# Feed-forward products of 512 tokens with their sums in two PSUM banks, and the chunk outputs of the attention part in the banks of the first product

## The chip, the cores and the metric

The program runs on one core of one Trainium2 chip. A core has TensorE (PE in the profile; its weight loads are listed apart as PEld), VectorE (DVE), ScalarE (ACT), GpSimd (POOL) and SyncE (SP, which issues all DMAs here). The metric is the time of one execution on the device, in microseconds.

## What is computed

A chunked state-space attention over 4 sequences of 768 tokens, with 8 heads of 32 channels, and then a feed-forward layer over the 3072 tokens (256 channels, 2048 hidden), all in float32:

```python
for c in range(nc):
    L = np.exp(cum[:, :, :, None] - cum[:, :, None, :]) * causal
    M = np.einsum('bhin,bhjn->bhij', Cc, Bc) * L
    y[:, :, sl] = einsum(M, xc) + einsum(Cc, state) * exp(cum)
    state = decay_full * state + sum(Bx)
x = y.transpose(0, 2, 1, 3).reshape(B * S, H * D)
h = x @ w_in
g = h - np.tanh(h)
return g @ w_out
```

## The kernel before

**Attention.** The tokens are cut into 28 chunks of up to 112 tokens (7 to a sequence, `CPB`). For each chunk, `chunk_a` makes decays and scores in PSUM (`att`, four banks, lines 452 and 458), ACT takes the exponential (`lt`, L462), DVE multiplies (L466) and POOL masks (L469). `chunk_y` makes the outputs `y` (L494) and the state for the next chunk (L502) in a PSUM bank of its own. ACT copies the state into the next chunk's `x` (L507, four small copies) and y into `xh` (L514), rounded to the type that PE multiplies in one pass; DVE keeps the rest, y - xh, in `xl` (L519).

**Feed-forward.** `TT` = 256 tokens make a window, `t` = 0 to 11. The 2048 hidden channels are eight units `u` of 256, each with its part of w_in and w_out, loaded as 64-bit words and converted by `conv` (five DVE and two ACT operations a unit) into a rounded weight `wh` and a rest `wl` (L321, the last of them). One step is one window with one unit. `mm1` makes `ph`, two blocks of 128 hidden channels by 256 tokens in one bank, as xh·wh + xh·wl + xl·wh over two halves of the 256 channels: 12 matmuls (L545). `act` does tanh (ACT, L559), subtracts (DVE, L563), rounds g to `gh` (ACT, L567) and keeps the rest `gl` (DVE, L574). `mm2` adds gh·wh + gh·wl + gl·wh into `o`, both halves of the output channels in one bank: 12 matmuls again (L595). There are two banks for `ph` (`NPH`), one for `o`, one for `y`, four for `att`: all eight.

**Sweeps.** Windows 0 to 3 go over the units two at a time (`SWEEPS`), because the units come one after another: at the end of a sweep `keep` adds `o` to a partial sum in SBUF (L609; a copy, L616, in the first sweep). Windows 4 to 11 take all eight units in a row. `store` empties the finished `o` (L627 with the partial sum; L629 on ACT and L631 on DVE, one half each, without) and sends it out (L634). That makes 96 steps.

**Order.** Nothing is issued as written. `Order` collects every operation with its engine, a cost and what it reads and writes; `slot` hands out buffers in turn, and an operation waits for those that read the buffer before. `plan` lists the operations by priorities that a seeded search varies, and `issue` emits them in the order of the planned starts, so each engine runs a fixed sequence. "hard" dependencies are waits with a latency, "soft" ones only an order.

Of the kernel before, what the change touches and what calls it, by code (L numbers as in the profile page):

```python
# [10 lines left out]
F32 = mybir.dt.float32  # L11
# [9 lines left out]
P = 128  # L21
# [9 lines left out]
TT = 256  # L31
NT = T // TT
# [12 lines left out]
SWEEPS = 0, 2, 4, 6, 8  # L45


class Order:
# [24 lines left out]
    def __call__(self, eng, cost, fn, r=(), w=(), dma=0, after=()):  # L73
# [134 lines left out]
def tile_ssm_moe(ctx: ExitStack, tc: tile.TileContext, a, x, bn, bc, wts, out):  # L208
# [16 lines left out]

    chunks, ends = {}, 0
    for t in range(NT):
        b, j = divmod(t, S // TT)
        end = b * CPB + -(-(j + 1) * TT // Q)
        chunks[t], ends = list(range(ends, end)), end  # L230
# [4 lines left out]
    SPAN = slice(len(chunks[0]), len(chunks[0]) + 7), slice(len(chunks[0]) + 7, NCK)  # L235
# [49 lines left out]
    wl = cp.tile([P, NCONV, 2, 2, 256], F32R, name="wl")  # L285

# [85 lines left out]
    def first_tile():  # L372
# [39 lines left out]
        for ck in range(len(chunks[0])):  # L412
# [65 lines left out]
    def chunk_y(ck):  # L478
# [4 lines left out]
        n_y = slot("y", 1)  # L483
# [6 lines left out]
        def fn():  # L490
            y = k["y"] = ps_y.tile([P, 2 * H * D], F32, tag="y", name=f"y{ck}")
# [17 lines left out]

        def fn_h():  # L510
            if c == 0:
                seq[b]["xh"] = p3.tile([P, 2, S], F32R, tag="xh", name=f"xh{b}", bufs=2)
            k["yv"] = k["y"][:, 0 : 2 * Q].rearrange("p (g q) -> p g q", g=2)[:, :, 0:q]
            nc.scalar.copy(seq[b]["xh"][:, :, c * Q : c * Q + q], k["yv"])  # L514

        def fn_l():
            if c == 0:
                seq[b]["xl"] = p3.tile([P, 2, S], F32R, tag="xl", name=f"xl{b}", bufs=2)
            nc.vector.tensor_tensor(out=seq[b]["xl"][:, :, c * Q : c * Q + q], in0=k["yv"],  # L519
                                    in1=seq[b]["xh"][:, :, c * Q : c * Q + q].bitcast(F32), op=ALU.subtract)  # L520
# [9 lines left out]
    def mm1(t, u):  # L530
        b, j = divmod(t, S // TT)
        d, ts = seq[b], slice(j * TT, (j + 1) * TT)
        cs = [c for c in range(CPB) if c * Q < ts.stop and (c + 1) * Q > ts.start]
        n_h, n_g = slot("ph", NPH), slot("g", 3)
        gs[t, u, 0] = [n_h, n_g]

        def fn():
            ph = ps_h.tile([P, 2, TT], F32, tag="ph", name=f"ph{t}_{u}")
            gs[t, u] = [ph]
            for j in range(2):  # L540

                for p in range(2):
                    for k in range(2):
                        for w_ in (wh, wl)[: 2 - p]:
                            nc.tensor.matmul(out=ph[:, j, :], lhsT=w_[:, u, 0, k, j * P : (j + 1) * P],  # L545
# [334 lines left out]
```

## Time and profile before

| | us |
|---|---|
| median of three runs | 345.87 |
| lowest and highest run | 345.47, 346.5 |
| span of the profiled execution | 344.3 |
| median less that span | 1.57 |
| busy: ACT | 192.9 |
| busy: POOL | 57.2 |
| mean granted TensorE clock | 0.970 |

The profile is one execution; its own time is not listed apart from its span, so the span is set against the median of the runs. A line of a group names its source line, engine and operation, output and inputs, the shape (partitions x elements) and the count, then busy us and mean ns of one, then the idle time before it and what ended it. Matmuls are pipelined: one lasts about 280 ns from start to end, and the next starts long before, so the pace is the distance of two starts, or a block's time divided by its count. The chain of waits is followed back from the last instruction.

### The profile page before, as it was taken

The numbers are of one execution on the slowest core, as the hardware profiler recorded it, in microseconds if no ns is written. First come the engines' busy times: TensorE is split into PE (matmuls) and PEld (weight loads), VectorE is DVE, ScalarE is ACT, GpSimd is POOL, SyncE is SP. The second block draws the span as 40 slices with busy tenths as digits, with TensorE's granted clock in tenths as the row PEclk, the third lists the DMA queues.
The fourth block names the chain that finished last, engine by engine and source line by source line (L and its number), as shares of the span: only waits on it lengthen the run. The fifth ranks groups of instructions, "written<-read, shape, count | busy, mean of one in ns | idle before, by whom it ended". The sixth has DMA issues, their size and how long they took to land.

```text
span 344.3 us, 8873 instructions
## 1 busy us (share of the span) xinstructions
PE 330.2 (96%) x3756; PEld 317.9 (92%) x3756; DVE 227.5 (66%) x339; ACT 192.9 (56%) x403; POOL 57.2 (17%) x69
## 2 busy tenths in 40 slices
PE   7939979999999999999999999999999999999995
PEld 6839879999999999999999999999999999999995
DVE  5996898999998875645654655555655555654552
ACT  7855977786554543534655646444554555554441
POOL 1544453340000110101211110210401110110000
PEclk9875989999999999999999999999999999999999
DMA  7929658614000011001211200200200100000100
GB/s 164 301 63 317 179 131 201 213 52 132 3 0 3 10 51 61 32 3 45 61 45 30 63 2 9 82 2 23 71 2 1 32 2 2 32 0 2 32 0 31
DMA packets 12471, 21.39 MB, mean 62 GB/s; under 512 B 2848, under 2 KB 7648, under 8 KB 12432
## 3 DMA queue, kind: packets, MB, share of 16 engines
q1 hardware_dynamic: 12432, 20.84, 21.4%
q8 instruction: 29, 0.48, 0.6%
q14 instruction: 10, 0.08, 0.1%
HBM read 17.51 MB, written 3.32 MB: 60 GB/s over the span
## 4 chain that ended last, share of the span: by engine, by line
PE 87%; DVE 3%; SPq 3%; DMA 3%; ACT 1%; issue 1%; POOL 0%; POOLq 0%; DVEq 0%; ACTq 0%
PE o L595 40%; PE ph L545 38%; PE y L494 3%; PE att L458 2%; DMA braw<-bn_d 2%; PE cp L381 1%; DMA bc<-bc_d 1%; PE att L452 1%; SPq L770 1%; SPq L278 1%; SPq L247 1%; PE y L502 1%; PE att L392 1%; DVE wm L310 0%; SPq L772 0%
## 5 line engine op out<-in xcount | busy, mean ns | idle before, releaser
L559 ACT ACTIVATE g<-ph 128x512 f32<-128x512 f32 x96 | 57.4, 598 | 91.5 <-PE ph L545 89.3
L563 DVE TENSOR_TENSOR g<-ph,g 128x512 f32<-128x512 f32 x96 | 65.9, 690 | 62.9 <-ACT g L559 62.9
L545 PE MATMUL ph<-xh,wh 128*128 128x256 f32 x384 | 101.3, 286 | 0.0
L545 PE MATMUL ph<-xh,wl 128*128 128x256 f32 x384 | 100.0, 283 | 0.0
L574 DVE TENSOR_TENSOR gl<-g,gh 128x512 fp32r<-128x512 f32 x96 | 67.0, 700 | 26.9 <-ACT gh L567 25.7
L545 PE MATMUL ph<-xl,wh 128*128 128x256 f32 x384 | 77.1, 282 | 0.0
L567 ACT CAST gh<-g 128x512 fp32r<-128x512 f32 x96 | 59.1, 619 | 28.7 <-DVE g L563 27.2
L545 PEld LDWEIGHTS ph<-xh,wh 128*128 128x128 f32 x384 | 73.8, 192 | 1.1 <-issue 0.4
L545 PEld LDWEIGHTS ph<-xh,wl 128*128 128x128 f32 x384 | 73.8, 192 | 0.0
L469 POOL TENSOR_SCALAR_AFFINE_SELECT lt<-lt 128x896 f32<-128x896 f32 (+1 forms) x25 | 34.0, 1359 | 203.9 <-DVE lt L466 203.9
L595 PE MATMUL o<-gh,wh 128*128 128x256 f32 x384 | 63.5, 287 | 0.0
L595 PE MATMUL o<-gl,wh 128*128 128x256 f32 x384 | 60.2, 278 | 0.0
L595 PE MATMUL o<-gh,wl 128*128 128x256 f32 x384 | 60.2, 278 | 0.0
L545 PEld LDWEIGHTS ph<-xl,wh 128*128 128x128 f32 x384 | 59.8, 192 | 0.0
L595 PEld LDWEIGHTS o<-gh,wh 128*128 128x128 f32 x384 | 51.2, 188 | 2.8
L595 PEld LDWEIGHTS o<-gl,wh 128*128 128x128 f32 x384 | 51.5, 188 | 0.0
L595 PEld LDWEIGHTS o<-gh,wl 128*128 128x128 f32 x384 | 51.5, 188 | 0.0
L466 DVE TENSOR_TENSOR lt<-att,lt 128x896 f32<-128x896 f32 (+1 forms) x25 | 26.7, 1067 | 6.8 <-ACT lt L462 6.8
L462 ACT ACTIVATE lt<-att 128x896 f32<-128x896 f32 (+1 forms) x25 | 22.6, 902 | 6.1 <-PE att L458 4.4
L507 ACT COPY x<-y 16x64 f32<-16x64 f32 x96 | 19.4, 202 | 8.6 <-DVE xl L519 7.1
L494 PE MATMUL y<-lt,x 128*32 128x112 f32 (+1 forms) x448 | 17.3, 274 | 5.4 <-POOL bc L352 3.3
L494 PEld LDWEIGHTS y<-lt,x 128*32 128x32 f32 x448 | 10.2, 113 | 9.2 <-POOL bc L352 3.4
(70 smaller groups left out, 232.8 us busy)
## 6 DMA issues: line engine op xcount, KB each, us to landing
raw<-w_d SPq DMA_DIRECT2D x16, 512.0 KB
x<-x_d SPq DMA_DIRECT2D x14, 256.0 KB
bc<-bc_d SPq DMA_DIRECT2D x56, 60.0 KB
out_d<-ob SPq DMA_DIRECT2D x24, 128.0 KB
braw<-bn_d SPq DMA_DIRECT2D x14, 112.0 KB
cum<-parts SPq DMA_DIRECT2D x1, 168.0 KB
rt_c<-cum SPq DMA_DIRECT2D x4, 27.0 KB
lt_c<-cum SPq DMA_DIRECT2D x4, 27.0 KB
```

The lines of the kernel that those rows point to most:

```text
L458: nc.tensor.matmul(out=at_[:, i, 2 + w, :], lhsT=bb[r, w], rhs=cc[r, w, 0:q], start=True, stop=True)
L462: nc.scalar.activation(k["l"][:, :, 0:q].rearrange("p (i w) q -> p i w q", i=4), k["a"][:, :, 0:2, :], AF.Exp)
L466: nc.vector.tensor_tensor(out=lt, in0=k["a"][:, :, 2:4, :], in1=lt, op=ALU.mult)
L469: nc.gpsimd.affine_select(out=k["l"][:, :, 0:q], in_=k["l"][:, :, 0:q], pattern=[[0, H], [1, q]], compare_op=ALU.is_ge, fill=0.0, base=N, ...
L494: nc.tensor.matmul(out=y[D * h : D * h + D, hg * Q : hg * Q + q], lhsT=d["x"][:, cg, P * hg + D * h : P * hg + D * h + D], rhs=k["l"][:, 4 ...
L507: nc.scalar.copy(grp[(ck + 1) // CPG]["x"][0:N, (ck + 1) % CPG, 2 * D * i : 2 * D * i + 2 * D], k["y"][D * i : D * i + N, H * D : H * D + ...
L545: nc.tensor.matmul(out=ph[:, j, :], lhsT=w_[:, u, 0, k, j * P : (j + 1) * P], rhs=d[("xh", "xl")[p]][:, k, ts], start=p == 0 and k == 0 an ...
L559: nc.scalar.activation(g, gs[t, u][0], AF.Tanh)
L563: nc.vector.tensor_tensor(out=g, in0=ph, in1=g, op=ALU.subtract)
L567: nc.scalar.copy(gh, gs[t, u][1])
L574: on.tensor_tensor(out=gl, in0=g, in1=gh.bitcast(F32), op=ALU.subtract)
L595: nc.tensor.matmul(out=po[t, seg][:, e, :], lhsT=w_[:, u, 1, j, e * P : (e + 1) * P], rhs=g[:, j, :], start=u == seg[0] and k == 0 and j = ...
```

## The change

Only the first sweep keeps windows of 256 tokens (`NARROW` = 1): 4 windows by 2 units, 8 steps. Everything else uses six windows of `TW` = 512 tokens. A wide step is one window with one block of 128 hidden channels, `f` = 0 to 15, so `ph` is still one bank: 128x512 instead of two blocks of 128x256. `mm1` and `mm2` of a wide step are 6 matmuls each. The sums of a wide window need two banks, one for each half of the output: the bank of `o` and the bank that `y` had, now also called `oe`. Chunks 10 to 27, which are not needed by the first 1024 tokens, therefore put `y` into one of the two banks of `ph`. A wide window crosses a sequence's end, so `xh` and `xl` become one tile each, with room for two sequences. Partial sums and outputs follow: two reads of 512 columns, on DVE for partial sums, on ACT and DVE without, and outputs of 256 KB instead of 128. In `Order`, a DMA that writes what another DMA wrote is now also ordered (soft) behind that DMA's issue.

```diff
-NT = T // TT
+TW = 512
+NARROW = 1
...
                 if dma and self.ops[j][0] == "DMA":
                     chain.add(j)
+                    soft.add(j - 1)
...
+    narrow = [(t * TT, TT) for t in range(NSW)]
+    wide = [(t * TW, TW) for t in range(T // TW)]
...
+    early = range(next(iter(chunks[wide[NSW * TT // TW]])))
...
+    xh = cp.tile([P, 2, 2 * S], F32R, name="xh")
+    xl = cp.tile([P, 2, 2 * S], F32R, name="xl")
...
-        n_y = slot("y", 1)
+        n_y = slot("y", 1) if ck in early else slot("ph", NPH)
...
-            y = k["y"] = ps_y.tile([P, 2 * H * D], F32, tag="y", name=f"y{ck}")
+            pool, tag = (ps_y, "y") if ck in early else (ps_h, "ph")
+            y = k["y"] = pool.tile([P, 2 * H * D], F32, tag=tag, name=f"y{ck}")
...
-    def mm1(t, u):
+    def mm1(w, f):
...
+        u, ts = f // 2, slice(at % (2 * S), at % (2 * S) + n)
+        blocks = range(f % 2, f % 2 + TW // n)
...
-            ph = ps_h.tile([P, 2, TT], F32, tag="ph", name=f"ph{t}_{u}")
-            for j in range(2):
+            ph = ps_h.tile([P, TW // n, n], F32, tag="ph", name=f"ph{at}_{f}")
+            for j in blocks:
...
-        op("PE", 1.41, fn, r=[*[d["n_xh"][c] for c in cs], *[d["n_xl"][c] for c in cs], f"wh{u}.0", f"wl{u}.0"], w=[n_h])
+        op("PE", 1.41 if n == TT else 1.32, fn,
...
-            n_po[t, seg] = slot("po", 1)
+            n_po[w, seg] = [slot("po", 1)] if n == TT else [slot("po", 1), slot("y", 1)]
...
+                    po[w, seg] = (ps_o.tile([P, TW], F32, tag="po", name=f"o{at}_{f}"),
+                                  ps_y.tile([P, TW], F32, tag="y", name=f"oe{at}_{f}"))
...
+        if n == TW:
+            for e in range(2):
+                op("DVE", 0.69, lambda e=e: nc.vector.tensor_tensor(out=partial(w)[:, e], in0=po[w, seg][e], in1=partial(w)[:, e], op=ALU.add),
...
+            for e in range(2):
+                op("DVE" if summed or e else "ACT", 0.69 if summed else 0.6, lambda e=e: fn_c(e),
...
-            op("SP", 0.42, lambda i=i: fn_d(i), r=[name[i]], dma=KB)
+            op("SP", 0.42, lambda e=e: fn_d(e), r=[name[e]], dma=KB * n // TT)
...
-    segs = [(t, tuple(range(i, j))) for i, j in zip(SWEEPS, SWEEPS[1:]) for t in range(NSW)]
-    segs += [(t, tuple(range(NCONV))) for t in range(NSW, NT)]
+    for s, (i, j) in enumerate(zip(SWEEPS, SWEEPS[1:])):
+        for w in narrow if s < NARROW else wide[: NSW * TT // TW]:
+            segs.append((w, tuple(range(2 * i, 2 * j, TW // w[1]))))
+    segs += [(w, tuple(range(NF))) for w in wide[NSW * TT // TW :]]
```

In these names a number behind ph, o, g, gh and gl is the window and the unit before (ph5_7 is window 5, unit 7), and the first token and the block f of the change (ph1024_7 is tokens 1024 to 1535, block 7); y16, lt16 and att17 are chunks; the last number only counts tiles. On PE, around the y of chunk 16, in the kernel before:

```order
L545 MATMUL ph5_7_2616<-xl1_797,wh_83 128x256 x2
L494 MATMUL y16_2633<-lt16_2579,x8_1208 32x112 x8
L502 MATMUL y16_2633<-x8_1208,bw8_1210 16x32 x8
L595 MATMUL o5_0_2414<-gh5_5_2582,wh_83 128x256 x4
L595 MATMUL o5_0_2414<-gh5_5_2582,wl_84 128x256 x4
L595 MATMUL o5_0_2414<-gl5_5_2598,wh_83 128x256 x4
L452 LDWEIGHTS lt_c_104
L452 MATMUL att17_2672<-rt_c_105,lt_c_104 128x224
```

There y16 has its own bank and stands between the end of a product and an o block of 12 matmuls. In the change, the same place on PE, from the last two matmuls of a product on:

```order
L553 MATMUL ph1024_7_1985<-xl_86,wh_83 128x512 x2
L502 MATMUL y16_1994<-lt16_1671,x8_1276 32x112 x8
L510 MATMUL y16_1994<-x8_1276,bw8_1278 16x32 x8
L611 MATMUL o1024_0_1876<-gh1024_5_1972,wh_83 128x512
L611 MATMUL oe1024_0_1877<-gh1024_5_1972,wh_83 128x512
L611 MATMUL o1024_0_1876<-gh1024_5_1972,wl_84 128x512
L611 MATMUL oe1024_0_1877<-gh1024_5_1972,wl_84 128x512
L611 MATMUL o1024_0_1876<-gl1024_5_1980,wh_83 128x512
L611 MATMUL oe1024_0_1877<-gl1024_5_1980,wh_83 128x512
L553 MATMUL ph1024_8_2028<-xh_85,wh_83 128x512
```

The o block is now six matmuls that alternate between the banks o and oe, and the product that follows it, ph1024_8, takes the ph bank of ph1024_7, since y16 holds the other one. The end of that product and what comes next on PE:

```order
L553 MATMUL ph1024_8_2028<-xl_86,wh_83 128x512 x2
L611 MATMUL o1024_0_1876<-gh1024_6_1992,wh_83 128x512
L611 MATMUL oe1024_0_1877<-gh1024_6_1992,wh_83 128x512
L611 MATMUL o1024_0_1876<-gh1024_6_1992,wl_84 128x512
L611 MATMUL oe1024_0_1877<-gh1024_6_1992,wl_84 128x512
L611 MATMUL o1024_0_1876<-gl1024_6_2011,wh_83 128x512
L611 MATMUL oe1024_0_1877<-gl1024_6_2011,wh_83 128x512
L553 MATMUL ph1024_9_2048<-xh_85,wh_83 128x512
```

So the bank of y16 is asked for again by ph1024_9, behind an o block, a product and another o block.

On DVE, around the last weight split (wl of unit 7, which reads wv7) in the kernel before:

```order
L609 TENSOR_TENSOR pt2_1029<-o2_4_1642,pt2_1029 128x512
L574 TENSOR_TENSOR gl3_5_1690<-g3_5_1655,gh3_5_1673 128x512
L321 TENSOR_TENSOR wl_84<-wv7_1395,wh_83 128x1024
L563 TENSOR_TENSOR g0_6_1705<-ph0_6_1675,g0_6_1705 128x512
L519 TENSOR_TENSOR xl1_797<-y11_1173,xh1_771 128x2x112
L466 TENSOR_TENSOR lt12_1170<-att12_1095,lt12_1170 128x896
L609 TENSOR_TENSOR pt3_1190<-o3_4_1692,pt3_1190 128x512
```

Here the xl of chunk 11 (it reads y11) and the lt of chunk 12 stand behind that split. In the change, on DVE, from the split of unit 6 on:

```order
L328 TENSOR_TENSOR wl_84<-wv6_1152,wh_83 128x1024
L573 TENSOR_TENSOR g512_8_1440<-ph512_8_1420,g512_8_1440 128x512
L309 TENSOR_SCALAR wm7_1452<-raw7_1182 128x1024
L473 TENSOR_TENSOR lt14_1394<-att14_1373,lt14_1394 128x896
L583 TENSOR_TENSOR gl0_10_1485<-g0_10_1386,gh0_10_1417 128x512
```

The lt of chunk 14 has come ahead of the last split, and those of chunks 12 and 13 stand earlier still. A little later on DVE the split of unit 7 itself:

```order
L525 TENSOR_TENSOR xl_86<-y12_1454,xh_85 128x2x112
L314 TENSOR_SCALAR wv7_1296<-wv7_1296 128x1024
L583 TENSOR_TENSOR gl512_9_1539<-g512_9_1504,gh512_9_1529 128x512
L632 TENSOR_TENSOR pt0_607<-o0_8_1432,pt0_607 128x512
L632 TENSOR_TENSOR pt0_607<-oe0_8_1433,pt0_607 128x512
L317 SCALAR_TENSOR_TENSOR wm7_1452<-wv7_1296,wm7_1452 128x1024
L321 SCALAR_TENSOR_TENSOR wv7_1296<-wv7_1296,wm7_1452 128x1024
L573 TENSOR_TENSOR g512_10_1549<-ph512_10_1532,g512_10_1549 128x512
L573 TENSOR_TENSOR g512_11_1562<-ph512_11_1542,g512_11_1562 128x512
L328 TENSOR_TENSOR wl_84<-wv7_1296,wh_83 128x1024
```

The xl of chunk 12 is ahead of it too, and each partial sum (pt) is now two operations, one for o and one for oe. The products of blocks 8 to 11, the third sweep, stand ahead of the split in both kernels.

More of the change, by code (lines that the diff above doesn't have):

```diff
@@ L224, in tile_ssm_moe @@
     raws, gs, po, n_po, obs, misc = {}, {}, {}, {}, {}, {}
+    narrow = [(t * TT, TT) for t in range(NSW)]
+    wide = [(t * TW, TW) for t in range(T // TW)]
     chunks, ends = {}, 0
[L227 to L230, printed above, removed]
+    for w in narrow + wide[NSW * TT // TW :]:
+        b, j = divmod(sum(w) - 1, S)
+        end = b * CPB + j // Q + 1
+        chunks[w], ends = list(range(ends, end)), end
     wv, wm, pts, n_pt = {}, {}, {}, {}
@@ L410, in fn_s @@
                                     fill=0.0, base=N, channel_multiplier=-1)
-        for ck in range(len(chunks[0])):
+        for ck in range(len(chunks[narrow[0]])):
             k = chs[ck]
@@ L567, in fn_h @@
[L567 to L568 removed]
+            gh = p3.tile(shape, F32R, tag="gh", name=f"gh{w[0]}_{f}")
+            nc.scalar.copy(gh, gs[w, f][1])
+            gs[w, f].append(gh)
         def fn_l():
[L571 to L575 removed]
+            _, g, gh = gs[w, f]
@@ L592, in fn @@
             for k, (w_, g) in enumerate(((wh, gh), (wl, gh), (wh, gl))):
-                for j in range(2):
+                for j in blocks:
                     for e in range(2):
-                        nc.tensor.matmul(out=po[t, seg][:, e, :], lhsT=w_[:, u, 1, j, e * P : (e + 1) * P],
-                                         rhs=g[:, j, :], start=u == seg[0] and k == 0 and j == 0 and e == 0,
-                                         stop=u == seg[-1] and k == 2 and j == 1, skip_group_check=True)
@@ L599, in mm2 @@
-        op("PE", 1.41, fn, r=[n_h, n_l, f"wh{u}.1", f"wl{u}.1"], w=[n_po[t, seg]])
-        if u == seg[-1]:
+                        nc.tensor.matmul(out=po[w, seg][e], lhsT=w_[:, u, 1, j, e * P : (e + 1) * P],
+                                         rhs=g[:, j - f % 2, :],
+                                         start=f == seg[0] and k == 0 and j == blocks[0] and (n == TW or e == 0),
+                                         stop=f == seg[-1] and k == 2 and j == blocks[-1], skip_group_check=True)
@@ L608, in keep @@
         if seg[0]:
-            op("DVE", 0.69, lambda: nc.vector.tensor_tensor(out=pts[t], in0=po[t, seg], in1=pts[t], op=ALU.add),
-               r=[n_po[t, seg]], w=[n_pt[t]])
+            op("DVE", 0.69, lambda: nc.vector.tensor_tensor(out=partial(w), in0=po[w, seg][2], in1=partial(w), op=ALU.add),
+               r=n_po[w, seg], w=[n_pt[i, e, half] for e in range(2)])
             return
-        n_pt[t] = slot("pt", NSW)
+        if half == 0:
+            names = op.pieces(slot("pt", NSW * TT // TW), 4)
+            n_pt.update({(i, e, x): names[2 * e + x] for e in range(2) for x in range(2)})
@@ L614, in fn @@
         def fn():
[L615 to L642 removed]
+            if half == 0:
+                pts[i] = p1.tile([P, 2, TW], F32, tag="pt", name=f"pt{i}", bufs=NSW * TT // TW)
@@ L824, in tile_ssm_moe @@
         if g < len(steps):
-            t, u, _ = steps[g]
-            mm1(t, u)
-            act(t, u, "DVE")
+            w, f, _ = steps[g]
+            mm1(w, f)
+            act(w, f)
             for fn, args in todo.get(g, ()):
```

151 lines of the change are left out of this document (83 added, 68 removed).

## The prediction

> **What bounds the kernel now.** I read the busy shares first, then the chain that ended last, then the span in stretches, then the instructions themselves where the bound sits.
>
> ```profile
> span 344.3 us, 8873 instructions
> PE 330.2 (96%) x3756; PEld 317.9 (92%) x3756; DVE 227.5 (66%) x339; ACT 192.9 (56%) x403; POOL 57.2 (17%) x69
> PE 87%; DVE 3%; SPq 3%; DMA 3%; ACT 1%; issue 1%; POOL 0%; POOLq 0%; DVEq 0%; ACTq 0%
> PE o L595 40%; PE ph L545 38%; PE y L494 3%; PE att L458 2%; DMA braw<-bn_d 2%; PE cp L381 1%; DMA bc<-bc_d 1%; PE att L452 1%; SPq L770 1%; SPq L278 1%; SPq L247 1%; PE y L502 1%; PE att L392 1%; DVE wm L310 0%; SPq L772 0%
> ```
>
> TensorE holds 87% of the chain, and the two feed-forward lines (L545 makes ph, L595 adds up o) hold 78% of it. The other engines and the DMA queues appear in the chain only near its start. The stretches show where that changes; each row gives busy us of PE, PEld (weight loads), DVE, ACT and POOL, then the granted clock.
>
> ```profile
> 20.00:30.00 10.00, 6.49 (x85) 5.75 (x85) 8.06 (x10) 4.79 (x13) 4.71 (x4) 0.54 0.54 166
> 50.00:60.00 10.00, 10.00 (x160) 9.42 (x159) 7.96 (x12) 6.66 (x17) 4.26 (x5) 0.93 0.74 177
> 60.00:75.00 15.00, 15.00 (x206) 14.16 (x205) 14.64 (x19) 11.62 (x26) 6.00 (x7) 1.00 0.43 134
> 75.00:118.00 43.00, 43.00 (x382) 43.00 (x381) 40.02 (x56) 24.32 (x42) 2.17 (x2) 1.00 0.11 35
> 118.00:200.00 82.00, 82.00 (x911) 79.64 (x914) 47.38 (x71) 41.36 (x87) 9.42 (x11) 1.00 0.14 42
> 200.00:340.70 140.70, 140.70 (x1556) 136.47 (x1548) 76.06 (x113) 70.76 (x145) 14.86 (x14) 1.00 0.06 18
> ```
>
> From 50 us to the last matmul PE has no idle time, and from 60 us its clock is full. Two kinds of stretch follow. From 60 to 118 us DVE is nearly as full as PE: 14.64 + 40.02 = 54.66 of 58 us, because it still converts weights. After 118 us DVE is at 54 to 58%, and PE alone decides. So what a PE instruction costs there is worth its full price.
>
> A busy PE says nothing of its pace; the chain's blocks do. One block is one product (mm1 or mm2) of one step, 12 matmuls of 256 columns.
>
> ```profile
> 78.89 1.36 PE o L595 x12
> ...
> 291.15 0.21 PE att L452 x4
> 291.35 0.45 PE att L458 x16
> 291.80 1.61 PE o L595 x12
> 293.41 1.41 PE ph L545 x12
> ...
> 297.65 0.52 PE y L494 x16
> 298.17 0.12 PE y L502 x16
> ```
>
> There are two paces: 1.36 / 12 = 113.3 ns and 1.41 / 12 = 117.5 ns per matmul. The chain's pieces from 75 us on hold 58 blocks of the first kind and 83 of the second, and 29 that follow attention work and pay about 0.2 us more (1.61 at 291.80). Mean of the first two kinds: (58 x 1.36 + 83 x 1.41) / 141 = 1.39 us, **116 ns per matmul, 232 ns per two**.
>
> **The change, part by part.** *Width.* Of the 96 steps, the 8 of the first sweep stay at 256 tokens; 88 become wide. Each had 24 matmuls of 256 columns and now has 12 of 512: 88 x 12 = 1056 pairs become one matmul each, with one weight load instead of two. The trace has no matmul of 512 columns. The lower bound of its time comes from a place where the clock was half.
>
> ```profile
> 49.00:51.20 2.20, 2.20 (x12) 2.20 (x12) 2.02 (x2) 1.22 (x5) 1.25 (x1) 0.50 0.14 38
> ...
> 48.99 0.42 PE L545 MATMUL ph<-xh,wl 128*128 128x256 f32 x1
> 49.21 0.41 PE L545 MATMUL ph<-xh,wh 128*128 128x256 f32 x1
> 49.42 0.41 PE L545 MATMUL ph<-xh,wl 128*128 128x256 f32 x1
> 49.63 0.63 PE L545 MATMUL ph<-xl,wh 128*128 128x256 f32 x2
> ```
>
> At clock 0.50 the same matmuls start (49.63 - 48.99) / 3 = 213 ns apart. If that is the stream of 256 columns alone, it takes 107 ns at the full clock, and the 113 to 118 measured there hold 6 to 11 ns of something else. What that is decides the price, and another row points at the weight load:
>
> ```profile
> 5.15 1.04 PE L381 MATMUL cp<-upto,la 128*128 128x112 f32 x8
> ```
>
> Here, at clock 1.00, eight matmuls of only 112 columns with the same 128x128 weights take 1.04 us; less the length of one (0.33 us, the group's mean), seven starts lie about 0.10 to 0.11 us apart. They are less than half as wide, and no faster. So I take it that near 110 ns the weight load sets the pace, that at 256 columns load and stream nearly tie, and that at 512 the stream stands alone. **Bounds for one wide matmul: 213 ns (stream alone) and 232 ns (as two now, no gain).** The half-clock rows are the nearest: they too stream for twice as long beside one load of the same weights. I take 216, 3 ns above them, since a full-clock pace never came down to its stream. Saving: 1056 x (232 - 216) = **-16.9 us**; by the bounds -20 and 0.
>
> The Trainium skill ("TensorE: Matmul & The Clock Gate", Back-to-back issue gap) gives a warm, isolated matmul N/2.4 + 2.5 ns, an estimate of 216 at 512 columns, by which the sum above would be the same. But the same rule gives 109 at 256: by it alone a pair costs 218 and the change saves 2.5 ns a pair, 2.6 us in all. This trace's 113 to 118 do not agree with that 109.
>
> *DVE in the sweeps.* Tanh, subtractions and casts stay as many and as long, 128x512 each:
>
> ```profile
> L563 DVE TENSOR_TENSOR g<-ph,g 128x512 f32<-128x512 f32 x96 | 65.9, 690 | 62.9 <-ACT g L559 62.9
> L574 DVE TENSOR_TENSOR gl<-g,gh 128x512 fp32r<-128x512 f32 x96 | 67.0, 700 | 26.9 <-ACT gh L567 25.7
> L466 DVE TENSOR_TENSOR lt<-att,lt 128x896 f32<-128x896 f32 x21 | 22.9, 1088 | 6.4 <-ACT lt L462 6.4
> L519 DVE TENSOR_TENSOR xl<-y,xh 128x224 fp32r<-128x224 f32 x24 | 9.3, 389 | 5.0 <-ACT x L507 3.8 <-ACT xh L514 1.1
> ```
>
> So DVE cannot follow where it is full. Between 60 us and the last weight split (unit 7) lie the sweeps over units 2 to 5, 16 steps: PE would gain 16 x 12 x 16 ns = 3.1 us. But the new order also puts the lt products of chunks 12 to 14 and the xl of chunks 11 and 12 ahead of that split on DVE (the order rows of the change show the last of them), which stood behind it: about 3 x 1.09 + 2 x 0.39 = 4.0 us, against the 58 - 54.7 = 3.3 us that DVE idles there. At best the split comes 0.7 us later than now, with about 2.0 us of PE's attention work done early (att of chunks 13 and 14 at 0.21 + 0.45, y of chunk 12 at 0.52 + 0.12, by the chain's rows above). So of the 3.1 us only 1.3 is realised, **+1.8**; if DVE keeps its idle time, +5.1. I take the first, since the planner has more to fill it with: **+2**.
>
> *y in the product banks.* 18 of the 28 chunks (10 to 27) put y into one of the two ph banks, and hold it until the last reader:
>
> ```profile
> 297.58 0.59 PE L494 MATMUL y<-lt,x 128*32 128x112 f32 x16
> 297.74 0.60 ACT L559 ACTIVATE g<-ph 128x512 f32<-128x512 f32 x1 [0.58 <-PE ph L545]
> 297.99 0.30 PE L502 MATMUL y<-x,bw 128*16 128x32 f32 x16
> 298.21 0.72 PE L595 MATMUL o<-gh,wh 128*128 128x256 f32 x4
> 298.37 0.69 DVE L563 TENSOR_TENSOR g<-ph,g 128x512 f32<-128x512 f32 x1 [0.48 <-ACT g L559]
> 298.61 0.41 ACT L507 COPY x<-y 16x64 f32<-16x64 f32 x2
> 299.05 0.39 DVE L519 TENSOR_TENSOR xl<-y,xh 128x224 fp32r<-128x224 f32 x1
> 299.48 0.20 ACT L507 COPY x<-y 16x64 f32<-16x64 f32 x1 [0.46 <-DVE xl L519]
> ```
>
> PE leaves y at about 298.29 and its last copy ends at 299.68, 1.4 us later. In the new order y is followed by an o block, a ph block into the other bank, and another o block before its own bank is wanted: about 3.9 us, enough. Tighter is the ph block right after: it wants the bank of the product ahead of y, which is read until tanh and subtraction are done, 299.06 against that product's end near 297.6: 1.5 us, where y and one o block give 0.64 + 1.30 = 1.94. Slack 0.4 us, unless another ACT or DVE instruction (lt, 0.9 to 1.1 us) stands ahead. Bounds: 0, and 18 x 0.7 = 12; behind a waiting matmul stands all of PE. I take the lower end's side, because this slack is positive: **+1.5** for this and for the sums below.
>
> *Two banks for the sum.* Fewer sums are emptied (14 instead of 24), each by two reads of 512 columns (0.69 us on DVE) instead of one of both halves. Most of the changeovers have two product blocks between the last and the next o block, 2.6 us of cover; where one stands there (1.3 us), the second bank is ready up to 0.3 us late. This is inside the 1.5.
>
> *The end.* The order still ends with four o blocks without a product.
>
> ```profile
> 335.11 5.67 PE o L595 x48
> 340.80 0.38 ACT ob L629
> 341.20 0.42 DVE ob L631
> ...
> GB/s 0 0 0 33 0 0 0 0 0 0 0 0 0 0 0 0 0 0 0 0 0 0 0 0 0 0 0 0 0 0 0 0 0 0 260 264 16 0 0 0
> ```
>
> Now ACT and DVE copy half each of one bank, one behind the other, 0.82 us; then two copies of twice the size from two banks can run together, 0.69. The last 256 KB moved at about 260 GB/s in slices of 0.5 us; 512 KB take 1.0 us more. **+1**.
>
> *Start.* The new soft rule on DMA writers reorders SP's queue and with it the first 50 us. PE idles 3.5 of 10 us between 20 and 30 us there, so it can go either way; I take 0, with 3 us to both sides.
>
> **Sum.** 344.3 - 16.9 + 2 + 1.5 + 1 = 331.9 us of span. The median of the runs, 345.87, is 1.6 above the profiled span; so **333.5 us**.
>
> **Rivals.** *A fixed price per matmul.* If the 6 to 7 ns over the stream at the faster pace belong to every matmul, a wide one takes 220, the saving falls by 1056 x 4 = 4.2 us: **337.7**. For it: the 113.3 recurs over long stretches. Against: the half-clock rows have no such part.
>
> *The price is in the columns.* If a wide matmul costs what two narrow ones do, 232, the 4.5 us of costs remain: **350.4**, slower. Point of decision: above 228 ns per wide matmul (4.5 / 1056 = 4 ns saved). The 112-column row speaks against it, as does the change of pace between 113 and 118 at equal columns. By the Trainium skill's fixed 2.5 ns (same page and section) this rival would save 2.6 us and end at 347.8.
>
> *The product banks become the bound.* If ACT serves y late, so that each of the 18 y costs PE the 1.4 us to its last reader, that is 25 us: 332.0 + 25 = **357**, slower. It decides from 13.9 / 18 = 0.8 us per y, twice the slack. For it: with y in a ph bank one bank is left for products. Against: ACT and DVE are half idle there (41.36 and 47.38 of 82 us).
>
> *DVE keeps its idle time in the sweeps, or the start is unlucky*: +3, **336.8**.
>
> **Chances.** Forecast 0.53; fixed price 0.24; DVE or start 0.12; columns 0.06; banks 0.05. The first three are faster, 0.89, and I leave 0.03 for the banks or columns ending within 0.3% of 345.87 (1.0 us, about what a measurement of this kernel can tell from no change), so 0.08 slower. Range: the forecast with 213 ns and a lucky start goes to 329; the fixed price with 3 us of bad start to 341. That leaves out columns, banks and a little of each tail.
>
> **What would show it.** The chain's blocks: six wide matmuls in 1.30 us (216), 1.32 (220) or 1.39 (no gain), with rows of 128x512 on L553 and L611. PE idle between 75 us and the end, with DVE ahead of it before unit 7's split, or with the readers of y behind ph. The time from the last o block to the end, 3.5 us now, at 4.5. I am wrong if blocks take over 1.37, if the granted clock falls under 1.00 after 60 us, or if PE idles over 5 us there.

## The result, and the profile after

| | before | after |
|---|---|---|
| median, us (17 runs each) | 344.55 | 346.68 |
| lowest and highest run, us | 343.66, 346.67 | 345.37, 348.91 |
| span of the profiled execution, us | 344.3 | 345.0 |

The ratio of the times is 1.0063, with a 95% interval of 1.0039 to 1.0087: the change makes the kernel slower by about 2 us, 0.6%. The forecast was 333.5 us with a range of 329 to 341, so it was wrong, in sign and size. The page of the kernel after, its first rows and its chain by engine and line:

```profile
span 345.0 us, 6725 instructions
PE 326.9 (95%) x2700; PEld 264.6 (77%) x2700; DVE 229.4 (66%) x335; ACT 194.6 (56%) x399; POOL 55.4 (16%) x69
PE 86%; DVE 5%; DMA 4%; ACT 2%; issue 1%; SPq 1%; ACTq 0%
PE ph L553 39%; PE o L611 21%; PE oe L611 18%; PE y L502 4%; PE att L465 3%; DMA x<-x_d 2%; DMA raw<-w_d 2%; PE att L459 1%; DVE lt L473 1%; DVE g L573 1%; ACT x L515 1%; DVE wl L328 1%; PE y L510 1%; DVE rt_c L437 1%; DVE wm L317 1%
```

PE has 1056 instructions less (2700 for 3756) and 53 us less of weight loads, but it is busy for 326.9 us instead of 330.2, and the two feed-forward lines still hold 78% of the chain. The weight loads that went had lain beside the matmuls. The stretches of the kernel after (length, then busy us and instructions of PE, PEld, DVE, ACT, POOL, then the granted clock):

```profile
20.00:60.00 40.00, 33.48 (x533) 30.34 (x533) 37.65 (x46) 28.03 (x61) 19.62 (x19) 0.83 0.67 185
60.00:75.00 15.00, 13.80 (x151) 12.39 (x152) 14.91 (x20) 11.63 (x25) 4.58 (x4) 1.00 0.45 137
75.00:118.00 43.00, 43.00 (x293) 33.63 (x292) 38.44 (x53) 26.01 (x47) 5.05 (x6) 1.00 0.16 46
118.00:200.00 82.00, 82.00 (x623) 64.72 (x622) 48.67 (x73) 42.09 (x89) 10.20 (x12) 1.00 0.11 35
200.00:341.00 141.00, 140.74 (x922) 111.36 (x920) 74.76 (x111) 69.28 (x134) 9.48 (x10) 1.00 0.05 16
```

From 75 us on PE idles for 141.00 - 140.74 = 0.26 us in all, at full clock, as before. So nothing new holds PE up there; what PE does there takes as long as it did. Blocks of one wide product in the chain, six matmuls each:

```profile
310.28 1.39 PE ph L553 x6
313.06 1.39 PE ph L553 x6
315.83 1.39 PE ph L553 x6
318.60 1.39 PE ph L553 x6
```

1.39 / 6 = 232 ns for one wide matmul; the mean distance of two starts, over 978 of them after 75 us (those across or right behind small matmuls are left out), is 230.8 ns. Two narrow ones cost 231.9 in the trace of before by the same count (115.97 over 2013). So a wide one saves 1.1 ns, not 16, and 1056 of them save **1.2 us**.

Two smaller places changed. Between 60 and 75 us PE now idles 1.20 us, where it was full. The rows around the second sweep's first product show it, in the timelines of after and of before:

```profile
65.07 0.68 DVE L573 TENSOR_TENSOR g<-ph,g 128x512 f32<-128x512 f32 x1
65.85 0.59 PE L502 MATMUL y<-lt,x 128*32 128x112 f32 x16 [0.76 <-issue]
66.23 0.33 PE L510 MATMUL y<-x,bw 128*16 128x32 f32 x16
66.27 0.68 DVE L573 TENSOR_TENSOR g<-ph,g 128x512 f32<-128x512 f32 x1
67.00 0.50 PE L553 MATMUL ph<-xh,wh 128*128 128x512 f32 x1 [0.45 <-DVE g L573]
```

```profile
65.01 0.38 PE L545 MATMUL ph<-xh,wh 128*128 128x256 f32 x1
```

It starts 2.0 us later. About 0.6 of that is one y, which stands ahead of it now (272 matmuls of y stand behind it in the kernel after and 288 in the kernel before, 16 a chunk, and one state fewer); 1.2 is the idle time, and 0.2 is not attributed. Both pieces of the idle time, 0.76 and 0.45, end just after a subtraction L573, at 65.75 and 66.95. This y is the eleventh, chunk 10, the first that takes a product bank: it waits until DVE has read the product that was there, and the wide product behind it waits for the other bank in the same way. (The profile puts the 0.76 down to "issue"; the wait ahead of y ends at 65.79 and is for two semaphores, of which DVE's had its last update at 65.76.) And the end, in the timeline of after:

```profile
340.34 0.40 PE L611 MATMUL oe<-gl,wh 128*128 128x512 f32 x1
340.54 0.59 ACT L666 COPY ob<-o 128x512 f32<-128x512 f32 x1 [3.73 <-PE o L611]
340.78 0.69 DVE L668 COPY ob<-oe 128x512 f32<-128x512 f32 x1 [3.23 <-PE oe L611]
```

From PE's last start to the end are 344.96 - 340.34 = 4.6 us; before, 344.31 - 340.48 = 3.8. The ledger of the two profiles: width -1.2, PE idle between 60 and 75 us +1.2, idle later +0.3, end +0.8, together +1.1; measured +0.7. The -0.4 that is left is not attributed. The medians lie 2.1 us apart and these two spans 0.7, since the profiled execution of before ran at a mean granted clock of 0.970 and that of after at 0.980, and executions at a lower clock are longer (before, about 346.5 us at 0.970 and 343.7 at 0.985).

### The profile page after: what moved, and what is told of

Same layout as the page of the kernel before. It is cut to its first block, busy times and chain, and to the rows that moved or that the text cites. A ratio compares the mean times of both kernels' runs of the same rounds, so it can differ in the third digit from the quotient of the medians.

```text
span 345.0 us, 6725 instructions
## 1 busy us (share of the span) xinstructions
PE 326.9 (95%) x2700; PEld 264.6 (77%) x2700; DVE 229.4 (66%) x335; ACT 194.6 (56%) x399; POOL 55.4 (16%) x69
## 4 chain that ended last, share of the span: by engine, by line
PE 86%; DVE 5%; DMA 4%; ACT 2%; issue 1%; SPq 1%; ACTq 0%
PE ph L553 39%; PE o L611 21%; PE oe L611 18%; PE y L502 4%; PE att L465 3%; DMA x<-x_d 2%; DMA raw<-w_d 2%; PE att L459 1%; DVE lt L473 1%; DVE g L573 1%; ACT x L515 1%; DVE wl L328 1%; PE y L510 1%; DVE rt_c L437 1%; DVE wm L317 1%
## 5 line engine op out<-in xcount | busy, mean ns | idle before, releaser
L573 DVE TENSOR_TENSOR g<-ph,g 128x512 f32<-128x512 f32 x96 | 66.0, 690 | 61.0 <-ACT g L569 60.6
L553 PE MATMUL ph<-xh,wh 128*128 128x512 f32 (+1 forms) x208 | 81.8, 395 | 0.4 <-DVE g L573 0.4
L553 PE MATMUL ph<-xh,wl 128*128 128x512 f32 (+1 forms) x208 | 79.5, 384 | 0.6 <-DVE wl L328 0.6
L553 PE MATMUL ph<-xl,wh 128*128 128x512 f32 (+1 forms) x208 | 61.8, 379 | 0.0
L553 PEld LDWEIGHTS ph<-xh,wl 128*128 128x128 f32 x208 | 40.6, 195 | 7.8 <-DVE wl L328 0.9
L611 PE MATMUL o<-gh,wh 128*128 128x512 f32 (+1 forms) x120 | 42.2, 384 | 0.0
L611 PE MATMUL o<-gh,wl 128*128 128x512 f32 (+1 forms) x120 | 39.6, 363 | 0.0
L611 PE MATMUL o<-gl,wh 128*128 128x512 f32 (+1 forms) x120 | 39.2, 359 | 0.0
L611 PE MATMUL oe<-gh,wh 128*128 128x512 f32 x88 | 34.7, 395 | 0.0
L611 PE MATMUL oe<-gh,wl 128*128 128x512 f32 x88 | 34.6, 394 | 0.0
L611 PE MATMUL oe<-gl,wh 128*128 128x512 f32 x88 | 34.6, 393 | 0.0
```

The lines of the kernel that those rows point to most:

```text
L553: nc.tensor.matmul(out=ph[:, j - f % 2, :], lhsT=w_[:, u, 0, k, j * P : (j + 1) * P], rhs=(xh, xl)[p][:, k, ts], start=p == 0 and k == 0 a ...
L573: nc.vector.tensor_tensor(out=g, in0=ph, in1=g, op=ALU.subtract)
L611: nc.tensor.matmul(out=po[w, seg][e], lhsT=w_[:, u, 1, j, e * P : (e + 1) * P], rhs=g[:, j - f % 2, :], start=f == seg[0] and k == 0 and j ...
```

## The experiments

**What a wide matmul costs by itself.** A kernel of nothing but streams of matmuls, each section 48 or 64 of one kind behind one another, the weights changing with each (but in one section):

```diff
+    for i in range(48):
+        mm(out=b[i % 4], lhsT=w[:, i % 4], rhs=x, start=True, stop=True)
+    for i in range(48):
+        mm(out=b[i % 4][:, 0:384], lhsT=w[:, i % 4], rhs=x[:, 0:384], start=True, stop=True)
...
+    for i in range(48):
+        mm(out=b[i % 4], lhsT=wb[:, i % 4], rhs=xb, start=True, stop=True)
```

> This kernel leaves the whole computation out: it only streams matmuls on TensorE, 48 or 64 of a kind in a row, weights of 128x128 loaded anew each time, into four PSUM banks in turn, and reads the pace. Kinds: fp32r with 512, 384, 256 and 128 columns, bf16 with 512 and 256, fp32r with 512 columns of zeros, 512 with the same weights again and again, all while the other engines are idle; then 512 and 256 columns while ACT and DVE work on SBUF. Theory A (the price is in the columns, about 0.443 to 0.460 ns each at the full clock, 6 to 10% over the 0.417 that the half-clock rows suggest): 512 at 227 to 235 ns, 384 at 170 to 177, 256 at 113 to 118, with or without ACT and DVE. Theory B (another engine's traffic slows the stream): 512 at 213 to 216 while the others idle, 227 to 235 once they work. Theory C (the operand's 4 bytes): fp32r at 227 to 235 but bf16 at 213 to 216. Theory D (the data, by way of the chip's power): zeros at 213 to 216, the rest at 227 to 235. If a price belonged to each matmul (the fixed price that the prediction gave 0.24), 512 less twice 256 would be negative by 6 ns or more.

Its sections in the timeline (start, then length, both in us; the pace is about the length less one matmul's own, over the count less one):

```profile
13.66 11.04 PE L55 MATMUL b<-x,w 128*128 128x512 f32 x48
24.54 8.51 PE L57 MATMUL b<-x,w 128*128 128x384 f32 x48
32.89 5.91 PE L59 MATMUL b<-x,w 128*128 128x256 f32 x48
38.63 5.47 PE L61 MATMUL b<-x,w 128*128 128x128 f32 x48
43.95 10.53 PE L63 MATMUL b<-xb,wb 128*128 128x512 bf16 x48
54.32 5.40 PE L65 MATMUL b<-xb,wb 128*128 128x256 bf16 x48
70.49 11.04 PE L69 MATMUL b<-x,w 128*128 128x512 f32 x48
```

By the starts themselves, over the last 24 of each section: 226.7 ns for 512 columns of the 4-byte operand, 173.3 for 384, 120.0 for 256, 111.7 for 128; in bf16 215.8 and 109.2. With one weight for all (L69), with zeros as data, or with ACT and DVE busy, 512 stay at 227. From 256 to 384 and from 384 to 512 columns the pace grows by 53.3 ns each time, 53.3 / 128 = 0.417 ns a column. That is just what the half-clock rows of before give when halved, 213 / 256 / 2. What is left is the same at all three widths: 226.7 - 213.3 = 173.3 - 160.0 = 120.0 - 106.7 = **13.3 ns for each matmul**, whatever its width; in bf16 it is 2.5. (Each matmul here has a weight load of its own, in L69 too, so the streams do not tell whether the 13.3 belong to the matmul or to its load.) At half clock nothing is left: 213 is 256 columns at twice 0.417. (At 128 columns the pace is 111.7 and not 66.7, so something else bounds it.) Of the expectations, the one on the operand's 4 bytes came true, that of 113 to 118 for 256 columns did not, and 512 columns less twice 256 is -13.3 ns, the sign of a price that belongs to each matmul.

In these terms the kernel before pays 106.7 + 6.7 or 106.7 + 10.8 for a narrow matmul, 106.7 + 9.3 in the mean, and the kernel after 213.3 + 17.5 for a wide one. A pair of narrow ones thus pays 18.6 above its columns and a wide one 17.5, hence the 1.1 ns. The kernels show neither the streams' 13.3 nor one price for each matmul, and the next experiments go at that.

**The width alone, within the new order.**

```diff
+                            for c in range(0, n, TT):
+                                cs_ = slice(ts.start + c, ts.start + c + TT)
+                                nc.tensor.matmul(out=ph[:, j - f % 2, c : c + TT], lhsT=w_[:, u, 0, k, j * P : (j + 1) * P],
+                                                 rhs=(xh, xl)[p][:, k, cs_], start=p == 0 and k == 0 and w_ is wh and c == 0,
+                                                 stop=p == 1 and k == 1, skip_group_check=True)
```

(The sums of mm2 likewise.)

> The changed kernel, with each wide matmul issued as two of 256 columns one after the other, on the same weights, into the same bank. All else (buffers, waits, planned order) stays. Theory A (the price is in the columns): the time of the changed kernel, 1.006 of the kernel before, within 0.3%; a pair at 227 to 235 ns. Rival (a price belongs to each matmul, and other losses of the change ate what it gained): 1056 x 6 to 16 ns more, 6 to 17 us, ratio 1.024 to 1.055.

355.38 us, ratio to before 1.0292 [1.0243, 1.0341]. The expectation of no change, if the price is in the columns, was missed; that of 1.024 to 1.055, if a price belongs to each matmul, came true. The chain's blocks say why:

```profile
323.84 1.45 PE ph L555 x12
326.70 1.45 PE ph L555 x12
329.56 1.45 PE ph L555 x12
```

1.45 / 12 = 121 ns, near the 120 of the streams; by the starts after 75 us the mean is 118.9, or 237.9 a pair. Against 230.8 for a wide one that is 7.1 ns x 1056 = 7.5 us, of the (1.0292 - 1.0063) x 344.55 = 7.9 us by which this kernel is slower than after. Width does buy time where two narrow matmuls cost 238 to 240. In the kernel before they cost 232, and there was next to nothing to buy. Read the other way, this kernel has all of the change but the width: that part costs 10 us, of which (118.9 - 116.0) x 2112 = 6.1 us are narrow matmuls that run slower in the new order. Why they do is open.

**The start: two parts of the change.** The new soft rule out of the kernel after, and the rule alone in the kernel before:

```diff
-                    soft.add(j - 1)
```

> The changed kernel without the added line of the planner (a DMA that follows another DMA into the same buffer is ordered behind its issue). Theory: the 2 us that the changed kernel has lost when its first wide product starts (67.0 us, against 65.0 us for the same product before) come from the new order of the DMA issues: without the line, about 2 us less, ratio near 1.000, and the first wide product near 65 us. Rival: the line does nothing for the time, the two planned starts differ by the luck of the search: a change of either sign, the rest of the span (first wide product to the end) the same 278 us as in the changed kernel.

```diff
+                    soft.add(j - 1)
```

> The kernel before with the planner's added line alone (a DMA that follows another DMA into the same buffer is ordered behind its issue); every width and buffer as before. Theory (this line's new plan of the first 60 us costs the changed kernel its late start): first feed-forward product of the second sweep 1 to 3 us later than in the kernel before, ratio 1.003 to 1.009. Rival (the late start is the width's doing, by the order of the first sweep): ratio 0.998 to 1.002.

Without the rule 349.5 us, 1.012 [1.0073, 1.0168], and the first wide product at 70.2 us, later than with it, against the expectation of 2 us less; from there to the end are 277.6 us, as in the kernel after (278.0). (This kernel leaves out an order of two DMAs into one buffer that its output needs, so its time tells of the plan alone.) With the rule alone 348.27 us, 1.0082 [1.005, 1.0113], and the second sweep at 66.6 us, 1.6 later than before, as expected. Both edits make it worse, so the rule has no price of its own that could be added up: every such edit makes the planner search anew, and over the kernels whose traces show it the second sweep starts anywhere from 60.9 to 70.2 us. Part of the second kernel's time is its pace: 116.8 ns a matmul for 116.0.

**Only the partial sums' windows narrow.**

```diff
-NARROW = 1
+NARROW = 4
```

> The changed kernel with all four sweeps at 256 tokens (NARROW = 4); only the windows from token 1024 on are wide, and chunks 10 to 27 still put y into the product's banks. Theory A: no width is worth anything, so the sweeps cost as before; the span from the first product of the third sweep to the end of the fourth is 46 to 47 us as before (88.2 to 134.5), and the total is 1.000 to 1.008, by what the start does. Rival (wide sums in two banks, or the attention drawn forward, cost time in the sweeps): 2 us or more faster than the changed kernel, below 1.000.

349.16 us, 1.0113 [1.0065, 1.0161]; second sweep at 68.2 us. From the first product of the third sweep to the first one behind the fourth pass 48.0 us here, all narrow, 46.8 in the kernel after with wide steps, and 46.3 in the kernel before, narrow again. The expected 46 to 47 us and at most 1.008 were both missed, since the narrow matmuls run at 118.9 ns here too, as with the halves. So in the new order wide steps are 1.2 us faster in these sweeps than narrow ones, and still no faster than the narrow ones of before.

**What sets the pace of the narrow ones.** Why do narrow matmuls run at 113.3 or 117.8 in before, and neither at the streams' 120? In that trace, from 65 us on, all 17 stretches behind the scores (`att`) of a chunk and the three behind a y alone run at 117.8, and 11 of the 13 behind the state matmuls (L502) at 113.3. So the theory was that the small forms ahead set the pace. First, streams behind each of these forms (here that of the state):

```diff
+    for i in range(8):
+        mm(out=at[32 * (i % 4) : 32 * (i % 4) + 16, 0, 0:32], lhsT=wf[:, 0:16], rhs=wf[:, 128:160], start=True, stop=True)
+    for i in range(36):
+        mm(out=b[i // 6 % 2][:, 0:256], lhsT=w8[:, i % 8], rhs=x2[:, i // 2 % 2, 0:256], start=i % 6 == 0, stop=i % 6 == 5, skip_group_check=True)
```

> Again only streams of matmuls, with the whole computation left out: 36 fp32r matmuls in a row, six added up in one bank as in the feed-forward products, first at 256 and 512 columns with nothing between, then 256 columns right after small matmuls of the forms that the attention part ends with (16x128 weights as in the scores; bf16 as in the decays; 32-column weights as in y; 16-column weights as in the state; one of the last form alone; scores and then one of the last form; scores and then bf16; y and then state), then 512 columns after decays and scores, and after y and state; at the end 96 of 512 and 96 of 256 while ACT and DVE read other PSUM banks. Theory P (the pace of the feed-forward stream is set by what stood on TensorE before it): 256 columns at 113 ns after 16-column weights, at 118 to 120 after the scores, 113 again when the 16-column form follows the scores. Rival (adding up in one bank, or ACT and DVE reading PSUM, costs the 4 to 5 ns): the same pace in all sections without readers, 118 or more for the one that adds up and 113 for the one that does not.

Then the kernel before with eight small matmuls added behind the scores (and behind the last y of a sequence):

```diff
+            settle(whole[:, 0, 4 * Q :])
...
+    def settle(room):
+        for w in range(2):
+            for i in range(4):
+                nc.tensor.matmul(out=room[32 * i : 32 * i + N, 32 * w : 32 * w + 32], lhsT=upto[:, 0:N], rhs=upto[:, 0:32],
+                                 start=True, stop=True)
```

> The kernel before (256 tokens everywhere), with eight small matmuls of the state's form (128x16 weights, 32 columns, results not used) behind each chunk's scores and behind a sequence's last y. In the kernel before, every feed-forward stretch that follows scores runs at 117.8 ns a matmul and 11 of 13 that follow the state's matmuls run at 113.3. Theory P: all stretches at 113.3; about 1250 matmuls gain 4.5 ns, 5.6 us, less 28 x 0.12 = 3.4 us for the added ones where nothing hides them: ratio 0.990 to 0.995. Rival (the pace follows something else, such as the time of the break): 117.8 stays after the scores, and the added matmuls cost 3 us: 1.008 to 1.010.

And the kernel before with the decays behind the scores:

```diff
-            for i in range(4):
-                r = slice(32 * i, 32 * i + 9)
-                nc.tensor.matmul(out=at_[:, i, 0:2, :], lhsT=lt_c[r, ck], rhs=rt_c[r, :, ck, N : N + q],
...
+            for i in range(4):
+                r = slice(32 * i, 32 * i + 9)
+                nc.tensor.matmul(out=at_[:, i, 0:2, :], lhsT=lt_c[r, ck], rhs=rt_c[r, :, ck, N : N + q],
```

> The kernel before, with the bf16 decay matmuls of each chunk behind the scores instead of ahead of them; no instruction more or less. Theory P, if any other form resets the pace: 113.3 after the attention, 5.6 us less, ratio 0.984. If only the 16-column form does: 117.8 as before, ratio 0.998 to 1.002.

The streams run at 120 and 227 in every section, whatever stands ahead. With the added matmuls 347.56 us, 1.0052 [1.0028, 1.0077], outside both ranges expected, and 16 of the 17 stretches behind the scores from 64 us on still run at 117.8; of the three behind a sequence's last y, two now run at 113.3. With the exchange 349.89 us, 1.0135 [1.0095, 1.0175], and from 67 us on every stretch runs at 117.2 to 117.8, those behind the state matmuls too. So the theory falls as it was put: the form right ahead does not set the pace. One thing goes with it: in before, in these two kernels and in that with the soft rule alone, the stretches behind the state matmuls from 62 us on run at 113.3 where their first two starts lie 221 to 223 ns apart, and at 117.2 to 117.8 where these lie 227 or 228 apart. So the pace is settled at the break and kept up to the next one; what settles it is open. Two more kernels of streams went at what makes a wide matmul cost 231 in the kernel and 227 in a stream: blocks that wait for another engine at their head, and the kernel's own operands, loops and banks. (In the blocks that wait, PE never stood idle; the wait was over each time.)

```diff
+        for j in range(6):
+            mm(out=b[i % 2], lhsT=w8[:, j % 8], rhs=xr[i % 2][:, 0:512], start=j % 6 == 0, stop=j % 6 == 5, skip_group_check=True)
+        nc.scalar.copy(xr[i % 2], b[i % 2])
```

> Streams only, the computation left out: 36 fp32r matmuls of 512 columns without waits; then blocks as in the feed-forward products, 6 of 512 or 12 of 256 columns, where ACT reads the bank behind each block, so that each block begins with a wait; the same with a moving operand that ACT writes anew for each block; then again 512 and 256 without waits. Alone and without waits 512 columns settle at 226.7 ns and 256 at 120. Theory W (a wait at a block's head disturbs the next few weight loads, and a block of six never settles): 512 columns at 229 to 232 ns in the blocks with waits, 226.7 without; 256 columns away from 120. Rival (waits are free, the 231 of the changed kernel has another source): 226.7 and 120 throughout.

```diff
+    for f in range(16):
+        i = 0
+        for p in range(2):
+            for k in range(2):
+                for w_ in (wh, wl)[: 2 - p]:
+                    mm(out=ph[f % 2], lhsT=w_[:, f // 2, 0, k, f % 2 * P : f % 2 * P + P], rhs=(xh, xl)[p][:, k, 512:1024], **st(i))
+                    i += 1
```

> Streams of matmuls alone; the whole computation is left out. What is open is the last 4 ns of the wide matmul: 231 ns in the kernel after, 226.7 in the streams so far, which all read one small weight tile. Here the operands lie as in the kernel (32 KB of wh and of wl, 12 KB of xh and of xl a partition, three tiles each of gh and gl). Sections of 36 at 512 columns: one weight and one operand; wh and wl in turn; a new weight address each time; xh and xl in turn; the product's loops; the sum's loops in two banks; then 16 steps of both, 192 matmuls; then 8 steps of both in halves of 256 columns, 192 matmuls; then the first section again. Theory (the price hangs on which operands follow one another): the 16 steps show 230 to 232 with the kernel's uneven gaps, 224 to 237 by the place in the block, and one of the four single sections shows the same, which names the operand; the halves show 113 to 118, not 120. Rival (operands don't matter, the rest of the kernel does): 226 to 228 in every section, 120 in the halves.

All of them settle at 226.7 and 120 again. The sums of the last kernel, in two banks in turn, in its timeline:

```profile
67.62 0.62 PE L67 MATMUL o<-gl,wh 128*128 128x512 f32 x2
68.07 0.62 PE L67 MATMUL o<-gh,wh 128*128 128x512 f32 x2
68.52 0.61 PE L67 MATMUL o<-gh,wl 128*128 128x512 f32 x2
68.98 0.39 PE L67 MATMUL o<-gl,wh 128*128 128x512 f32 x1
```

(68.98 - 67.62) / 6 = 227, with the banks, tiles and order of the kernel, in which it is 231. So none of these makes the difference by itself in a stream: zeros as data, the operands' places, the banks, a wait at a block's head, the forms ahead. What does stays open. It is worth 1056 x 4.1 ns = 4.3 us of the missing saving. The larger part, (226.7 - 216) x 1056 = 11.3 us, is what the streams show: 13.3 ns above the columns where the forecast had 3.

**The planner's price.** The planner orders the work by a cost of 1.32 us for a wide block, 220 ns a matmul, and 1.41 for a narrow one. Both measure 1.39. With the measured price:

```diff
-        op("PE", 1.41 if n == TT else 1.32, fn,
+        op("PE", 1.39, fn,
```

> The changed kernel with the planner's cost of a block of products at 1.39 us for both widths (measured: 1.39 before, 1.385 after; the change has 1.41 and 1.32). Theory L (the first 67 us come out differently with every new plan, by one or two us either way, and no part of the change sets that): first wide product anywhere from 63 to 70 us, ratio 0.997 to 1.015. Rival (the planner's wrong price costs the changed kernel its late start): first wide product at 65 us or earlier and ratio 1.000 or less.

With that price and another seed of the search:

```diff
-    ROUNDS, JITTER, SEED, CLIMB, RAMP = 16, 0.3, 133908, 1500, 110.0
+    ROUNDS, JITTER, SEED, CLIMB, RAMP = 16, 0.3, 6, 1500, 110.0
```

> As the run before, with another seed of the planner's search, the one of eight whose plan it rates best (by 1.1 us). Theory L: its rating says little; ratio 0.997 to 1.015. Rival (the plan is what the planner says): 1.1 us below the run before. If it starts the wide products by 64 us, the whole would come out below the kernel before, ratio 0.997 to 1.000, since from there on the wide kernel needs about a microsecond less.

And with another seed alone, at the old prices:

```diff
-    ROUNDS, JITTER, SEED, CLIMB, RAMP = 16, 0.3, 133908, 1500, 110.0
+    ROUNDS, JITTER, SEED, CLIMB, RAMP = 16, 0.3, 1, 1500, 110.0
```

> The changed kernel with another seed alone. Theory L: first wide product 1 to 3 us away from 67.0, and the time follows; from the first wide product to TensorE's end 272 to 276 us as in the changed kernel (273.3). Rival (start and rest hang together, the rest varies as much): that stretch differs by 3 us or more.

With the price 341.84 us, ratio to before 0.991 [0.988, 0.9941]; with it and seed 6, 341.47, 0.990 [0.9852, 0.9947]; with seed 1 alone 346.58, 1.004 [1.0016, 1.0064]. With the price both ratios lie below the 0.997 of theory L, and the rival's 1.000 or less came true; the 1.1 us between the two seeds did not come. The other seed alone starts the wide products at 67.2 us, 0.2 from the 67.0 and not 1 to 3, and needs 273.2 us from there, as expected. That is two seeds with each price (346.68 and 346.58 with the old one): in these four the price decides, not the seed. Four plans are few, and seed 6 was picked from eight by its rating. The stretches of the kernel with the price and seed 6:

```profile
20.00:60.00 40.00, 35.63 (x584) 32.32 (x588) 39.18 (x51) 32.10 (x72) 21.73 (x21) 0.92 0.79 219
60.00:75.00 15.00, 15.00 (x133) 12.55 (x126) 13.68 (x18) 11.28 (x21) 2.98 (x3) 1.00 0.41 129
```

and its second sweep's first product:

```profile
60.85 0.50 PE L553 MATMUL ph<-xh,wh 128*128 128x512 f32 x1
```

By 60 us PE has done 584 matmuls since 20 us, where after has 533 and before 532 in the same time, and then it does not idle. The product starts 6.1 us earlier than in after. From there to PE's last start are 334.0 - 60.9 = 273.1 us; in after 340.3 - 67.0 = 273.3. So the whole gain lies ahead of the second sweep, and nothing behind it moved. Part of it goes with the clock: between 20 and 60 us it was 0.92 here and 0.83 in after, worth up to 0.09 x 40 = 3.6 us. The clock alone is not the gain: at a mean granted clock of 0.975 an execution of the kernel with the price alone took 343.6 us, and those of after 346.4 to 347.0. That kernel has no trace from which its start can be read. This version beats both kernels; that it does so by an earlier second sweep and not by the width is what these numbers show. Why a price of 1.32 leads the search to the poorer start was not tried, nor were other prices or seeds for the kernel before, which might gain as much.

## Why the prediction was wrong

**The price of a wide matmul is the step that failed.** Its saving came out 15.7 us smaller, -1.2 for -16.9, and the other terms 2.6 us lower than forecast, which makes the 13.1 us between the span forecast, 331.9, and the 345.0 measured. The step read the 213 ns of 256 columns at clock 0.50 as "the stream of 256 columns alone" and halved it for the full clock: 107 for 256, 213 for 512. So far it holds, since the streams show 0.417 ns a column at full clock, the half of 213 / 256. What failed is what it put on top. It took the "6 to 11 ns of something else" of a narrow matmul for the weight load, which a wide stream would hide, and left 3 ns for a wide one. Measured are 13.3 ns above the columns in the streams, at 256, 384 and 512 columns alike, and 17.5 in the kernel after. The half-clock rows have no such part, so they gave the columns rightly and hid the rest. The 112-column row was rightly read (128 columns take 111.7 in the streams, hardly less than 256 do), but it proves only that narrow matmuls are held at some 110 ns, not that the load was what held the 256 columns. Of the 14.8 ns by which 230.8 lies over 216, the streams show 10.7; the other 4.1, and why the narrow ones of before paid less than 13.3, stay open.

The Trainium skill ("TensorE: Matmul & The Clock Gate", Back-to-back issue gap) gives N/2.4 + 2.5 ns warm and N/1.2 cold for an isolated matmul. The bf16 streams agree with the first to 1 ns (216 and 109), the half-clock rows with the second (213), and the 4-byte streams at full clock do not (226.7 and 120 for 215.8 and 109.2). The forecast's caution, that the same rule gives 109 at 256 and so a saving of only 2.6 us, was nearest to the 1.2 measured. The streams have the shape of that rule, a price per column and one per matmul, but the second is 13.3; the kernel's saving does not follow from either.

**The rival "the price is in the columns"** had the number and not the mechanism; it had been given 0.06. Its point of decision, 228 ns, lies under the measured 230.8, and its sign was right. But the columns cost the 0.417 ns of the forecast, and a wide matmul comes near two narrow ones because of what is paid above them, 17.5 and 18.6 ns. Its time, 350.4, was 3.7 us too high: 1.3 because the median of before is 344.55 over 17 runs and was 345.87 over three, and 2.4 because the change cost 2.1 us and not 4.5. **The rival "a fixed price per matmul"** (0.24) named what the streams show, at half its size, 6 to 7 ns for 13.3; its 220 was wrong too, and so was its argument against itself, that the half-clock rows have no such part.

**DVE in the sweeps, +2, and y in the product banks with two banks for the sum, +1.5:** together 1.5 us of idle PE came, 1.20 between 60 and 75 us and 0.26 from 75 us on. The 1.20 belong to both: the first y in a product bank and the product behind it wait for that bank, and DVE gives it free late. From 75 to 118 us, where I had placed most of DVE's term, PE is full; there was no gain for DVE to hold back. Behind the first one, the y in the product banks are almost free, and the slack of 0.4 us held.

**The end, +1:** right; 0.8. The two copies overlap as the step said (340.54 and 340.78).

**The start, 0 with 3 to both sides:** the second sweep is 2.0 us late, inside the bounds. What was missed is its cause. I named the soft rule; the runs without it and with it alone show no price of its own. What the traces show are the waits of the first y and of the product behind it for their banks, and one y that has moved ahead. What brought the start forward, by 6.1 us, was the planner's price for a block, with seed 6. A forecast that takes a stage built by a search as fixed had no term for that.

Two sums of the forecast are slightly off, and neither touches the outcome: 213 ns with 3 us of luck at the start gives 327 and not 329, and 333.5 + 3 is 336.5 and not 336.8.

## What to carry to other kernels

One pace at one width is not a price per column. Two or three widths, at the clock that counts, give the column's price as the slope and show what is paid for each matmul as the rest; here that rest was 13.3 ns in the streams and 17.5 in the kernel, where the forecast had 3. A pace at half clock gave the slope rightly and hid the rest. Before a matmul is made wider to save weight loads, see whether the loads lie beside the stream; a PE that is full says nothing of that, and a drop of 53 us in loads brought 1.2 us. Where a search orders the work by prices, measure the new block and put its price in: with two seeds at each price that was worth some 5 us here, four times what the width was.

## What the runs showed of the hardware

- At the full clock a stream of 4-byte matmuls with 128x128 weights takes 226.7 ns for 512 columns, 173.3 for 384 and 120 for 256: 0.417 ns a column and 13.3 ns for each matmul. In bf16 it takes 215.8 for 512 and 109.2 for 256, the same 0.417 a column and 2.5.
- The same 4-byte operand costs 213 ns for 256 columns at clock 0.50, and 120 (streams) or 113 to 118 (kernel) at 1.00. Doubling the clock shortens it by 1.78 to 1.88 and not by 2.
- In the streams 128 columns take 111.7 ns and 256 take 120, so below about 256 columns narrowing a matmul saves almost nothing here.
- Behind small forms the second 128x128 matmul starts some 105 ns late: the first two starts lie 223 ns apart for a pace of 120 and 335 for 227.
- Identical blocks of narrow matmuls run at 113.3 or at 117.8 ns in one execution for tens of us at a time, and at neither of them alone (120). No stream, with the forms ahead, the waits, the operands or the banks of the kernel, settles at these two paces, and no cause was found.
